# Attention and FFN in one kernel: score visits of three or four blocks, FFN tiles evicted once, and an order that keeps VectorE and GpSimd adds apart

## The chip, the core and the metric

The kernel runs on one core of a Trainium2 chip. TensorE (PE) multiplies matrices into PSUM, VectorE (DVE) and ScalarE (ACT) read PSUM and SBUF, GpSimd (POOL) reads SBUF, SyncE (SP) issues most DMAs. The metric is the device time of one launch in microseconds (us): the median of three runs.

## The reference

One layer, 2048 tokens of 640 values, no batch:

```python
xn = _layernorm(x, axis=-1)
return x + _A_ref(xn, A_wq, A_wk, A_wv, A_wo) + _B_ref(xn, B_w1, B_w2)
```

`_A_ref` is attention with 32 query heads of 20 values and one shared key and value head: `softmax(q k^T / sqrt(20)) v`, then `wo`. `_B_ref` is `silu(xn w1) w2` with 1728 hidden values.

## The kernel before, in words

**Tiling.** A score block is 128 keys by 512 queries of one head, transposed (keys on partitions). There are 4 chunks of 512 queries, 32 heads and 16 key tiles, so 2048 blocks. Four heads make a group, of 64 blocks; there are 32 groups. PSUM has eight banks of 512 fp32 columns. Two sets of three (banks 0 to 5) take score blocks in turn, bank 6 (`UBANK`) gathers the output of the group in work, bank 7 (`XBANK`) is the job bank: every other matmul tile of the loop goes through it, one at a time.

**A score visit** (`do_S`) multiplies three blocks side by side in row strips of PE (L823). ACT then exponentiates two of them in one instruction (L841), or all three. The third, where `want_dve` allows it, goes to DVE: a clamp from PSUM to 16-bit integers (L856, `p1`), whose bits read as bf16 approximate the exponential. Two more versions with an added constant refine it (`flush_z`): up to three clamped blocks make a set, the second version is made on POOL (L888), the first on DVE (L882) or POOL, by a comparison of their queues. So a DVE block costs three products with the values in place of one. A PV slot (`do_pv`, L762) multiplies one item for each of the four heads of the group, side by side in column strips of PE.

**Jobs** are the remaining matmul tiles: query tiles (`qd_job`, L977, emptied by DVE at L984), FFN first-layer tiles (`h_job`, L1013; ACT computes tanh of half the value at L1026, and DVE the product `(tanh + 1) * value` at L1031, both reading bank 7), FFN second layer and output projection (`out_job`, L1081 and L1086, emptied by DVE at L1098, L1104 or L1116). `fill_chunk` hands them out, with a first step each from `PACE` and `AHEAD`.

**Order.** The program is planned on the host. `Sched.run` simulates the five engines with fixed prices (`t_act`, `t_dve_ps` and others) and latencies, and writes down an order of instructions for each; the chip runs those lists, with semaphores for the data dependencies alone. On DVE, ACT and POOL the planner takes the ready instruction of the lowest `prio`. On PE, `step` chooses among a score visit (first, when its banks and operands are ready), a PV slot, a job matmul and a filling matmul of zeros; `PV_PRESS` and `PV_GO` say when PV comes first. A `lock`ed instruction of DVE isn't planned to start while a locked one of POOL runs, and the other way round; before, the DVE adds, normalisations and some of the start are locked, the POOL adds are not:

```python
        if op.lock:
            r = max(r, self.lock_end["pool" if op.eng == "dve" else "dve"])
```

**Start and end.** `prologue` loads x, computes the layer norm (statistics on DVE and ACT, norms on the engines of `NORM_ENG`), transposes it by DMA (tiles in `DT`, issued from SP) or on PE (`PRO`), and makes keys and values. After the last score block, leftover jobs and the last output projection remain.

Of the kernel before, what the change touches and what calls it, by code (L numbers as in the profile page):

```python
# [14 lines left out]
P = 128  # L15
# [32 lines left out]
ZB = 3  # L48
LATE_G = 0
AHEAD = 30  # L50
Q_FROM = 8
H0_STEP = 14
Y_SLOW = 0.1
# [4 lines left out]
ZWAIT = 6  # L58
SWITCH = 0.105
S_LEAD = 0.56  # L60
PV_PRESS = 8
DVE_TH = 3.4
U_PRIO = 1.1
X_PRIO = 0.8
PACE = (0.9, 0.9, 0.9, 0.9)
# [4 lines left out]
OVER = 0.1  # L70
PV_HOLD = 29
Q_EVERY = 2
DT_ISSUE = 1.28
UT_ISSUE = 1.05
DT = (4, 5, 6, 9, 10, 11, 12, 13, 14, 15)
NORM_P = 4.5
DVE_FROM = 8
NODB = 2
GB = 4 * KT
NB = NUNITS * KT  # L80
Y0_POOL = 1.0
Y0_COST = 1.45
YP_FIX = 0.14
YP_BLK = 0.47
PV_MIN = 4
PV_GO = 5
PRO = "v0 t7 t8 v1 k2 k3 k4 k5 v2 k6 k7 v3 q1 d0"
ACT_STATS = (4, 6, 9, 12, 14)
NW_ENG = ("dve", "dve", "dve")
NORM_ENG = ("pool", "pool", "pool", "pool", "act", "pool", "act", "act", "dve", "act", "act", "act")  # L90
# [256 lines left out]
def t_mm(n):  # L347
    return max(n, 64) / 2400.0 + 0.003
# [18 lines left out]
class Builder:  # L367
# [17 lines left out]
    def alloc(self):  # L385
# [21 lines left out]
        self.tb = sb([P, 2, QW], BF16)  # L407
        self.qo = sb([P, QW], BF16)
# [47 lines left out]
    def steps_init(self):  # L456
        self.NG = NUNITS // 4
        self.T = -(-NB // 3)
        self.s_next = 0
        self.misc = deque()  # L460
# [14 lines left out]
        self.cg = 0  # L475
        self.g_seen = [0] * self.NG
# [16 lines left out]
    def blocks(self, t):  # L493
        return [(b // GB, b % GB // 4, b % 4) for b in range(3 * t, min(3 * t + 3, NB))]

    def more(self):
        return (self.s_next < self.T or self.cg < self.NG or bool(self.misc) or bool(self.pro) or bool(self.urgent)
                or self.cur_job is not None)

    def bank_for_job(self, job=None):  # L500
# [8 lines left out]
        if self.s_next >= self.T:  # L509
            banks = [b for b in (7, 0, 1, 2, 3, 4, 5) if b not in self.heldb.values()]  # L510
# [31 lines left out]
    def s_reads(self, t, dv):  # L542
        k = []
        for g, kt, j in self.blocks(t):
            c, h = g // 8, 4 * (g % 8) + j
            k += [("kT1" if dv else "kT", kt // 2), ("kT", kt // 2), ("qb", c % 2, h)] + self.qkeys(c, h)
# [8 lines left out]
    def s_ready(self, t):  # L555
        r = self.reads_ready(self.s_reads(t, False))
# [4 lines left out]
        nh = len(self.blocks(t))  # L561
# [10 lines left out]
    def step(self, now):  # L572
        sc = self.sc
        t = self.s_next
        sr = INF
        if t < self.T:
            sr = self.s_ready(t)
            if sr <= now + 1e-9:
                self.do_S(t, now)
# [23 lines left out]
        if pv_n and (self.pe_mode == "PV" or press):  # L603
# [12 lines left out]
        if self.s_next >= self.T - LASTPV and (pv_n or self.s_next >= self.T and pv_some):  # L616
# [3 lines left out]
        if choice == "PV":  # L620
            d = 0.216 + self.switch("PV")
# [25 lines left out]
    def fill(self, now, until):  # L647
        if self.s_next >= self.T and self.cg >= self.NG:
# [936 lines left out]
```

## Time and profile before

| | before |
|---|---|
| time, median of three runs | 739.06 us (738.4 to 739.63) |
| profiled execution: time / span | 740.91 us / 738.9 us |
| busy of the span: PE, DVE, ACT, POOL | 709.2, 659.1, 695.0, 489.8 us |
| score exps (L841) | 683, 658.1 us |
| clamps (L856) | 653, 433.2 us |
| DVE adds (L882) / POOL adds (L888) | 150, 131.5 us / 292, 446.6 us |
| mean granted TensorE clock | 0.992 |

The span runs from the first to the last instruction of the core; the time holds the launch around it too. A group line gives the source line, engine, operation, what is written and read, the count, the busy time, the mean duration in ns, and the idle time of the engine just before with what ended it. Durations of neighbours on one engine overlap, so counts times means exceed what an engine needs. A wait line says who waited for whom, the total, the times, and the longest.

### The profile page before, as it was taken

The page shows a single profiled execution, that of the slowest core. Times are in us where ns is not written, and L with a number is a line of the kernel's source. Part 1 is how long each engine was busy: PE and PEld are TensorE (multiplying, and loading weights), DVE is VectorE, ACT ScalarE, POOL GpSimd, SP SyncE. Part 2 cuts the span into 40 slices and gives each one's busy share as a digit, 9 for nine tenths or more (in the row PEclk, how much of TensorE's full clock was granted, in tenths as well). Part 3 has the DMA queues.
Part 4 walks back from the last instruction along what each step waited for, and adds up shares of the span by engine and source line. Part 5 has one row for each costly group of instructions (what it writes and reads, how often), then busy time and mean ns, then how long its engine had stood idle before and what let it go on. Part 6 is the DMA issues. An engine that isn't in the chain of part 4 may idle for free.

```text
span 738.9 us, 17791 instructions
## 1 busy us (share of the span) xinstructions
PE 709.2 (96%) x6661; PEld 223.8 (30%) x6661; DVE 659.1 (89%) x1106; ACT 695.0 (94%) x775; POOL 489.8 (66%) x366
## 2 busy tenths in 40 slices
PE   9899999999999999999999999999999999999998
PEld 4422222233332322223333232222333223223334
DVE  6679989989998899999989899999998999999993
ACT  6979999999999999999999999999999999999990
POOL 3356766766777766767677676756775777566770
PEclk9979999999999999999999999999999999999999
DMA  9525310000010101000011011000001002000011
GB/s 283 113 84 154 110 15 19 12 16 16 9 45 9 43 25 34 20 19 8 8 11 43 8 59 37 16 16 16 8 2 43 10 8 62 27 8 1 9 37 36
DMA packets 52554, 27.69 MB, mean 37 GB/s; under 512 B 38422, under 2 KB 51830, under 8 KB 52470
## 3 DMA queue, kind: packets, MB, share of 16 engines
q1 hardware_dynamic: 51014, 26.35, 13.3%
q8 instruction: 54, 0.88, 0.5%
q10 hardware_dynamic: 1456, 0.22, 0.2%
q14 instruction: 30, 0.25, 0.1%
HBM read 11.44 MB, written 2.62 MB: 19 GB/s over the span
## 4 chain that ended last, share of the span: by engine, by line
PE 58%; DVE 19%; issue 11%; POOL 8%; ACT 3%; DMA 0%; POOLq 0%; DVEq 0%
PE psall L823 19%; PE psall L762 18%; DVE sbt L856 11%; PE psall L1081 9%; POOL sbt L888 8%; PE psall L1013 5%; DVE sbt L882 5%; PE psall L977 2%; PE psall L684 2%; PE psall L1086 1%; ACT sbt L841 1%; DVE sbt L1031 1%; ACT sbt L1362 1%; DVE sbt L931 1%; DVE sbt L1116 1%
## 5 line engine op out<-in xcount | busy, mean ns | idle before, releaser
L841 ACT ACTIVATE sbt<-psall 128x1024 bf16<-128x1024 f32 (+1 forms) x683 | 658.1, 1071 | 19.7 <-PE psall L823 16.3
L888 POOL TENSOR_TENSOR sbt<-sbt 128x768 int32<-128x768 int32 (+1 forms) x292 | 446.6, 1546 | 202.2 <-DVE sbt L856 158.6
L856 DVE TENSOR_SCALAR sbt<-psall 128x512 int16<-128x512 f32 x653 | 433.2, 682 | 49.0 <-PE psall L823 41.5
L823 PE MATMUL psall<-sbt 32*128 32x512 bf16 x2048 | 268.2, 386 | 15.9 <-DVE sbt L856 10.9
L762 PE MATMUL psall<-sbt 128*32 128x512 bf16 x3354 | 263.8, 386 | 4.6 <-DVE sbt L931 2.3
L823 PEld LDWEIGHTS psall<-sbt 32*128 32x128 bf16 x2048 | 68.2, 91 | 255.6 <-issue 98.0
L882 DVE TENSOR_SCALAR sbt<-sbt 128x1536 int16<-128x1536 int16 (+1 forms) x150 | 131.5, 876 | 2.7
L762 PEld LDWEIGHTS psall<-sbt 128*32 128x32 bf16 x3354 | 65.0, 94 | 119.4 <-issue 76.0
L1081 PE MATMUL psall<-sbt 128*128 128x320 bf16 x448 | 88.6, 303 | 0.0
L1013 PE MATMUL psall<-sbt 128*128 128x512 bf16 x260 | 79.2, 384 | 1.6 <-DVE sbt L1031 0.4
L1081 PEld LDWEIGHTS psall<-sbt 128*128 128x128 bf16 x448 | 34.3, 97 | 45.2 <-issue 33.1
L1031 DVE SCALAR_TENSOR_TENSOR sbt<-sbt,psall 128x512 bf16<-128x512 bf16 x54 | 36.6, 677 | 2.4 <-PE psall L823 1.1
L1026 ACT ACTIVATE sbt<-psall 128x512 bf16<-128x512 f32 x54 | 33.9, 628 | 0.2 <-DVE sbt L882 0.2
L977 PE MATMUL psall<-sbt 128*128 128x512 bf16 (+1 forms) x95 | 28.9, 385 | 0.6 <-DVE sbt L1031 0.6
L1086 PE MATMUL psall<-sbt 128*128 128x320 bf16 x144 | 29.1, 303 | 0.3 <-DVE sbt L1116 0.3
L920 POOL TENSOR_TENSOR sbt<-sbt 128x320 bf16<-128x320 bf16 x31 | 26.8, 865 | 3.8 <-DVE sbt L915 3.4
L1013 PEld LDWEIGHTS psall<-sbt 128*128 128x128 bf16 x260 | 17.1, 97 | 37.0 <-issue 22.2
L931 DVE CAST sbt<-psall 128x512 bf16<-128x512 f32 x32 | 21.8, 680 | 2.1 <-PE psall L762 2.1
L684 PE MATMUL psall<-sbt 128*128 128x512 bf16 (+2 forms) x76 | 20.3, 420 | 1.5 <-POOL sbt L1281 1.5
L1482 POOL TENSOR_SCALAR sbt<-sbt 128x256 bf16<-128x256 bf16 x8 | 4.1, 514 | 23.4 <-DVE sbt L1480 23.3
L1098 DVE SCALAR_TENSOR_TENSOR sbt<-psall,sbt 128x320 bf16<-128x320 f32 x28 | 13.5, 484 | 4.6 <-PE psall L1081 4.2
L1116 DVE SCALAR_TENSOR_TENSOR sbt<-psall,sbt 128x320 bf16<-128x320 f32 x28 | 13.2, 480 | 3.1 <-PE psall L1086 3.1
(81 smaller groups left out, 160.9 us busy)
## 6 DMA issues: line engine op xcount, KB each, us to landing
sbt<-in_A_x_dram SPq DMA_DIRECT2D x32, 160.0 KB, 3.4
out_dram<-sbt SPq DMA_DIRECT2D x15, 160.0 KB, 1.8
sbt<-in_B_w_dram SPq DMA_DIRECT2D x5, 432.0 KB, 6.3
sbt<-sbt SPq DMA_DIRECT2D x105, 20.0 KB
sbt<-in_B_w_dram SPq DMA_DIRECT2D x13, 160.0 KB, 3.0
sbt<-sbt SPq DMA_DIRECT2D x1, 1024.0 KB, 6.0
sbt<-sbt SPq DMA_TRANSPOSE x57, 2.4
sbt<-in_A_wo_dram SPq DMA_DIRECT2D x5, 160.0 KB, 2.7
```

The costliest lines, as they stand in the source:

```text
L684: return pe.matmul(self.bk(b, 0, n), self.zero[:, 0:P], self.zero[:, 0:n], start=True, stop=True)
L762: ins = pe.matmul(self.bk(UBANK, 0, QW, r, r + SLOT), self.v[:, it.w, it.kt, :], it.x(), start=f, stop=False, tile_position=(0, r), skip_g ...
L823: ins = pe.matmul(self.bk(par3 + i), self.kT[r:r + SLOT, kk, kt * P:(kt + 1) * P], self.qT[r:r + SLOT, g % 8, (g // 8) % 2, :], start=True ...
L841: return a.activation(self.E[:, b0 * QW:(b0 + na) * QW], self.ps[:, par3 * BANK:(par3 + na) * BANK], AF.Exp, scale=ACT_SCALE)
L856: return v.tensor_scalar(self.Z[:, zs, zp * QW:(zp + 1) * QW], self.bk(bb), 0.0, ZMAX, ALU.max, ALU.min)
L882: sc.new("dve", td, lambda v, k=k: v.tensor_scalar(self.Y[:, zs, k, 0:w], self.Z[:, zs, 0:w], float(PH[k + 1][0]), None, ALU.add), zk, yk, ...
L888: sc.new("pool", tp, lambda v, k=k, cb=cb: v.tensor_tensor(self.Y[:, zs, k, 0:w].bitcast(I32), self.Z[:, zs, 0:w].bitcast(I32), cb, ALU.ad ...
L977: return pe.matmul(self.bk(b, 0, QW, 0, rows), self.wq[:, k, lo:hi], self.xnT[:, k, c * QW:(c + 1) * QW], start=(k == 0), stop=(k == DC - 1))
L1013: return pe.matmul(self.bk(b), self.w1[:, k, fk * P:(fk + 1) * P], self.xnT[:, k, c * QW:(c + 1) * QW], start=(k == 0), stop=(k == DC - 1))
L1031: sc.new("dve", t_dve_ps(QW), lambda v: v.scalar_tensor_tensor(out=self.hT[0:rows, fk, :], in0=t, scalar=1.0, in1=src, op0=ALU.add, op1=AL ...
L1081: return pe.matmul(self.bk(b, 0, 320), self.hT[r0:r1, fk, i * P:(i + 1) * P], self.w2[r0:r1, fk, e0:e0 + 320], start=(m == 0), stop=(m == ...
L1086: return pe.matmul(self.bk(b, 0, 320), self.oT[:, k, i * P:(i + 1) * P], self.wo[:, k, e0:e0 + 320], start=(m == 0 and src != "ps"), stop= ...
```

## The change

A score visit takes a fourth block when the job bank is free, no job is open and at least one block of the four goes to DVE (`x_free`, `do_S`). `pick_dve` replaces `want_dve`: it may choose any of the visit's blocks, by how few blocks of that head DVE has taken (at most `TILE_CAP`), one in a visit of three and up to two in one of four, each below a bound on DVE's queue. In a visit of four, bank 7 holds a DVE block. The last two blocks of a group are no longer kept from DVE (`NODB` is 0).

An FFN tile is copied by DVE from bank 7 to a bf16 buffer `hb` in SBUF; tanh and the product read that buffer. POOL adds are locked as DVE adds are. A begun job goes on before PV (`JOB_BURST`). Sets are flushed after 3 visits in place of 6. In the start, the zero tile is set by DVE, tile 8 is transposed by DMA and tile 14 on PE, two norms leave ACT, and filling matmuls up to 5.6 us are priced at half speed. Prices, pacing and priorities of the planner are changed. What is left out below counts blocks (`bp`) and visits (`nv`) in place of steps.

```diff
@@ -47,47 +47,55 @@
-AHEAD = 30
-Q_FROM = 8
-H0_STEP = 14
-Y_SLOW = 0.1
+AHEAD = 31
+Q_FROM = 11
+H0_STEP = 18
+Y_SLOW = 0.085
-ZWAIT = 6
+ZWAIT = 3
-PV_PRESS = 8
+PV_PRESS = 2
-U_PRIO = 1.1
-X_PRIO = 0.8
-PACE = (0.9, 0.9, 0.9, 0.9)
+U_PRIO = 1.8856
+X_PRIO = 0.2256
+PACE = (0.85, 0.8, 0.75, 0.95)
-OVER = 0.1
-PV_HOLD = 29
-Q_EVERY = 2
+COLD = 5.6
+TILE_CAP = 10
+FOUR_FROM = 46
+JOB_BURST = 3
+TH_PRIO = 0.883
+DVE_TH2 = 0.562
+HP_PRIO = 5.8323
+FOUR_LAST = 4
+OVER = 0.0939
+PV_HOLD = 25
+Q_EVERY = 3
-DT = (4, 5, 6, 9, 10, 11, 12, 13, 14, 15)
-NORM_P = 4.5
-DVE_FROM = 8
-NODB = 2
+DT = (4, 5, 6, 8, 9, 10, 11, 12, 13, 15)
+NORM_P = 3.5
+DVE_FROM = 6
+NODB = 0
-Y0_POOL = 1.0
-Y0_COST = 1.45
-YP_FIX = 0.14
-YP_BLK = 0.47
+Y0_POOL = 1.1547
+Y0_COST = 1.5225
+YP_FIX = 0.185
+YP_BLK = 0.426
-PRO = "v0 t7 t8 v1 k2 k3 k4 k5 v2 k6 k7 v3 q1 d0"
+PRO = "v0 t7 k3 v1 k2 q1 k4 k5 v2 t14 k6 k7 v3 d0"
-NORM_ENG = ("pool", "pool", "pool", "pool", "act", "pool", "act", "act", "dve", "act", "act", "act")
+NORM_ENG = ("pool", "pool", "pool", "pool", "dve", "pool", "act", "act", "dve", "pool", "act", "act")
...
@@ -345,7 +353,7 @@
-    return max(n, 64) / 2400.0 + 0.003
+    return max(n, 64) / 2400.0 + (0.008 if n > 400 else 0.006 if n > 300 else 0.003)
...
         choice = None
-        if pv_n and (self.pe_mode == "PV" or press):
+        if JOB_BURST and job is not None and job.begun and not press:
+            choice = "M"
+        elif pv_n and (self.pe_mode == "PV" or press):
             choice = "PV"
...
-        if self.s_next >= self.T and self.cg >= self.NG:
+        if self.bp >= NB and self.cg >= self.NG:
-        room = min(until, now + 0.33) - now - self.switch(mode)
+        room = (min(until, now + (0.66 if now < COLD else 0.33)) - now - self.switch(mode)) / (2.0 if now < COLD else 1.0)
-        op = sc.new("pe", n / 2400.0 + self.switch(mode), fn, [("zero",)], [ukey] if ukey else [],
-                    name="fill", queue=False)
+        op = sc.new("pe", n / 2400.0 * (2.0 if now < COLD else 1.0) + self.switch(mode), fn, [("zero",)],
+                    [ukey] if ukey else [], name="fill", queue=False)
-        op.work = 0.216
+        op.work = 0.2215
...
@@ -792,46 +808,80 @@
         self.tq[g][tile].append(it)
         self.e_used += na
 
-    def want_dve(self, t):
-        g, kt, j = self.blocks(t)[-1]
-        if t < DVE_FROM or 4 * kt + j >= GB - NODB or t >= self.T - DVE_LAST:
-            return False
+    def pick_dve(self, bs, most):
+        t = self.s_next
+        if t < DVE_FROM or t >= self.T - DVE_LAST:
+            return []
         sc = self.sc
         back = sc.t["dve"] - sc.t["pe"]
         for op in sc.pend["dve"]:
             back += op.dur
         back += len(self.zblocks) * 0.6
-        return back < DVE_TH
-
-    def do_S(self, t, now):
+        got = []
+        cand = [x for x in bs if 4 * x[1] + x[2] < GB - NODB and self.nz[x[0]][x[2]] < TILE_CAP
+                and self.reads_ready([("kT1", x[1] // 2)]) <= sc.t["pe"] + 1e-9]
+        cand.sort(key=lambda x: (self.nz[x[0]][x[2]], -bs.index(x)))
+        for x, th in zip(cand, (DVE_TH, DVE_TH2)):
+            if back >= th or len(got) == most:
+                break
+            got.append(x)
+        return got
+
+    def x_free(self, now):
+        if self.cur_job is not None or not self.pv_started or self.pro_left:
+            return False
+        for d in self.sc.deps_of((), [("B", XBANK)]):
+            if d.avail is None or (d.avail if d.eng != "pe" else d.end) > now + 1e-9:
+                return False
+        return True
+
+    def do_S(self, now):
         sc = self.sc
-        bs = self.blocks(t)
-        nh = len(bs)
+        t = self.s_next
         self.started = True
         for c in range(QC):
             if c not in self.filled and t >= self.first_step[c] - AHEAD:
                 self.filled.add(c)
                 self.fill_chunk(c, t)
-        dv = self.want_dve(t)
-        par3 = 3 * (t % 2)
+        bs = self.blocks()
+        four = False
+        if len(bs) == 3 and t >= FOUR_FROM and t < self.T - FOUR_LAST and self.x_free(now):
+            b4 = self.blocks(4)
+            if len(b4) == 4 and self.reads_ready(self.s_reads(b4)) <= now + 1e-9:
+                dvs = self.pick_dve(b4, 2)
+                four = bool(dvs)
+        if four:
+            bs = b4
+        else:
+            dvs = self.pick_dve(bs, 1)
+        nh = len(bs)
+        par3 = 3 * (self.nv % 2)
+        acts = [x for x in bs if x not in dvs]
+        na = len(acts)
+        bank = {x: par3 + i for i, x in enumerate(acts)}
+        for x, bb in zip(dvs, (XBANK, par3 + na) if four else (par3 + na,)):
+            bank[x] = bb
 
         def fn(pe):
             ins = None
-            for i, (g, kt, j) in enumerate(bs):
+            for x in bs:
+                g, kt, j = x
                 r = j * SLOT
-                kk = 1 if (dv and i == nh - 1) else 0
-                ins = pe.matmul(self.bk(par3 + i), self.kT[r:r + SLOT, kk, kt * P:(kt + 1) * P],
+                kk = 1 if x in dvs else 0
+                ins = pe.matmul(self.bk(bank[x]), self.kT[r:r + SLOT, kk, kt * P:(kt + 1) * P],
                                 self.qT[r:r + SLOT, g % 8, (g // 8) % 2, :],
                                 start=True, stop=True, tile_position=(r, 0))
             return ins
-        op = sc.new("pe", 0.216 + self.switch("S"), fn, self.s_reads(t, dv), [("B", par3 + j) for j in range(nh)],
+        op = sc.new("pe", 0.216 + self.switch("S"), fn, self.s_reads(bs, dvs), [("B", bank[x]) for x in bs],
                     name=f"S{t}", queue=False)
         op.mm = nh
         op.work = 0.216
         self.pe_mode = "S"
-        self.s_next = t + 1
+        self.bp += nh
+        self.s_next = self.bp // 3 if self.bp < NB else self.T
+        v = self.nv
+        self.nv += 1
         sc.commit(op, now)
-        na = nh - 1 if dv else nh
         if self.blk_pos + na > NBLK:
             self.blk_pos = 0
         b0 = self.blk_pos
@@ -840,28 +890,31 @@
         def efn(a):
             return a.activation(self.E[:, b0 * QW:(b0 + na) * QW],
                                 self.ps[:, par3 * BANK:(par3 + na) * BANK], AF.Exp, scale=ACT_SCALE)
-        self.exp_op[t] = sc.new("act", t_act(na * QW), efn, [("B", par3 + j) for j in range(na)],
+        self.exp_op[v] = sc.new("act", t_act(na * QW), efn, [("B", par3 + j) for j in range(na)],
                                 [("E", b0 + j) for j in range(na)], prio=5.0, name=f"exp{t}")
-        for i in range(na):
-            g, kt, j = bs[i]
+        for i, (g, kt, j) in enumerate(acts):
             self.item(g, j, kt, 0, lambda b=b0 + i: self.E[:, b * QW:(b + 1) * QW], [("E", b0 + i)], 1)
             self.g_seen[g] += 1
-        if dv:
+        for x in dvs:
             self.dve_steps += 1
-            g, kt, j = bs[-1]
+            g, kt, j = x
+            self.nz[g][j] += 1
             zs, zp = self.zset, len(self.zblocks)
-            bb = par3 + nh - 1
-
-            def p1(v):
+
+            def p1(v, zs=zs, zp=zp, bb=bank[x]):
                 return v.tensor_scalar(self.Z[:, zs, zp * QW:(zp + 1) * QW], self.bk(bb), 0.0, ZMAX,
                                        ALU.max, ALU.min)
-            sc.new("dve", t_dve_ps(QW), p1, [("B", bb)], [("Z", zs, zp)], prio=1.0, name=f"p1_{t}")
-            self.item(g, j, kt, 0, lambda: self.Z[:, zs, zp * QW:(zp + 1) * QW].bitcast(BF16), [("Z", zs, zp)])
+            sc.new("dve", t_dve_ps(QW), p1, [("B", bank[x])], [("Z", zs, zp)], prio=0.9 if bank[x] == XBANK else 1.0,
+                   name=f"p1_{t}")
+            self.item(g, j, kt, 0, lambda zs=zs, zp=zp: self.Z[:, zs, zp * QW:(zp + 1) * QW].bitcast(BF16),
+                      [("Z", zs, zp)])
             self.g_seen[g] += 1
             self.g_late[g] += 1
-            self.zblocks.append((t, g, kt, j))
-        if self.zblocks and (len(self.zblocks) >= ZB or t - self.zblocks[0][0] >= ZWAIT or t == self.T - 1
-                             or 3 * (t + 1) >= GB * (self.zblocks[0][1] + 1)):
+            self.zblocks.append((v, g, kt, j))
+            if len(self.zblocks) >= ZB:
+                self.flush_z()
+        if self.zblocks and (v - self.zblocks[0][0] >= ZWAIT or self.bp >= NB
+                             or self.bp >= GB * (self.zblocks[0][1] + 1)):
             self.flush_z()
 
     def flush_z(self):
@@ -887,7 +940,7 @@
             cb = bass.AP(self.cy, c.offset, [list(c.ap[0]), [0, w // 2]])
             sc.new("pool", tp, lambda v, k=k, cb=cb: v.tensor_tensor(
                 self.Y[:, zs, k, 0:w].bitcast(I32), self.Z[:, zs, 0:w].bitcast(I32), cb, ALU.add), zk + [("cy",)], yk,
-                prio=4.0, name=f"yp{k}")
+                prio=4.0, name=f"yp{k}").lock = True
         for i, (t, g, kt, j) in enumerate(self.zblocks):
             for k in range(2):
                 self.item(g, j, kt, k + 1, lambda k=k, i=i: self.Y[:, zs, k, i * QW:(i + 1) * QW].bitcast(BF16),
@@ -1023,14 +1076,17 @@
             tp = fk % 2
             t = self.tb[0:rows, tp, :]
             src = self.bk(b, 0, QW, 0, rows)
-            sc.new("act", t_act(QW), lambda a: a.activation(t, src, AF.Tanh, scale=0.5), [("B", b)], [("tb", tp)],
-                   prio=X_PRIO, name=f"th{c}_{fk}")
+            hb = self.hb[0:rows, tp, :]
+            sc.new("dve", t_dve_ps(QW), lambda v: v.tensor_copy(hb, src), [("B", b)], [("hb", tp)], prio=X_PRIO,
+                   name=f"hc{c}_{fk}")
+            sc.new("act", t_act(QW), lambda a: a.activation(t, hb, AF.Tanh, scale=0.5), [("hb", tp)], [("tb", tp)],
+                   prio=TH_PRIO, name=f"th{c}_{fk}")
             ks = [("hT", fk)]
             if c == 0:
                 ks += [("hT_x", i) for i in range(fk * QW // D, min(self.XS - 1, (fk * QW + QW - 1) // D) + 1)]
-            sc.new("dve", t_dve_ps(QW), lambda v: v.scalar_tensor_tensor(
-                out=self.hT[0:rows, fk, :], in0=t, scalar=1.0, in1=src, op0=ALU.add, op1=ALU.mult),
-                [("B", b), ("tb", tp)], ks, prio=X_PRIO, name=f"hp{c}_{fk}")
+            sc.new("dve", t_dve_1x(QW), lambda v: v.scalar_tensor_tensor(
+                out=self.hT[0:rows, fk, :], in0=t, scalar=1.0, in1=hb, op0=ALU.add, op1=ALU.mult),
+                [("hb", tp), ("tb", tp)], ks, prio=HP_PRIO, name=f"hp{c}_{fk}")
...
-        pool(0.3, lambda g: g.memset(self.zero[:, :], 0.0), [], [("zero",)])
+        np_("dve", 0.3, lambda v: v.memset(self.zero[:, :], 0.0), [], [("zero",)], prio=-1.0, name="zero")
```

## The prediction

> **What bounds the kernel now.** I read the page's busy shares first, then its chain and groups by shape, then the waits, then stretches of the timeline.
>
> ```profile
> PE 709.2 (96%) x6661; PEld 223.8 (30%) x6661; DVE 659.1 (89%) x1106; ACT 695.0 (94%) x775; POOL 489.8 (66%) x366
> ...
> PE 58%; DVE 19%; issue 11%; POOL 8%; ACT 3%; DMA 0%; POOLq 0%; DVEq 0%
> ```
>
> Three engines are nearly full and the chain runs through all of them, so a change must relieve PE, ACT and DVE together. The groups by shape give the prices:
>
> ```profile
> L841 ACT ACTIVATE sbt<-psall 128x1024 bf16<-128x1024 f32 x654 | 620.9, 1053 | 19.0 <-PE psall L823 15.9 <-ACT sbt L841 0.4
> L856 DVE TENSOR_SCALAR sbt<-psall 128x512 int16<-128x512 f32 x653 | 433.2, 682 | 49.0 <-PE psall L823 41.5 <-POOL sbt L888 0.9
> L888 POOL TENSOR_TENSOR sbt<-sbt 128x768 int32<-128x768 int32 x280 | 432.9, 1563 | 198.9 <-DVE sbt L856 155.3 <-PE psall L823 26.4 <-issue 4.1
> ...
> L882 DVE TENSOR_SCALAR sbt<-sbt 128x1536 int16<-128x1536 int16 x142 | 123.8, 872 | 2.5
> ...
> L841 ACT ACTIVATE sbt<-psall 128x1536 bf16<-128x1536 f32 x29 | 42.0, 1466 | 0.6 <-PE psall L823 0.5
> L1031 DVE SCALAR_TENSOR_TENSOR sbt<-sbt,psall 128x512 bf16<-128x512 bf16 x54 | 36.6, 677 | 2.4 <-PE psall L823 1.1 <-ACT sbt L1026 1.0
> L1026 ACT ACTIVATE sbt<-psall 128x512 bf16<-128x512 f32 x54 | 33.9, 628 | 0.2 <-DVE sbt L882 0.2
> ```
>
> Durations overlap their neighbours, so I price by median start-to-start times of back-to-back instructions, taken from the trace: exp of two blocks 0.904 us, of three 1.330; clamp (L856) 0.601; eviction of 512 columns (L931) 0.598; tanh 0.477; silu product (L1031) 0.595. From the exps, a block costs ACT 0.426 and a visit 0.052 more. So the number of visits hardly matters to ACT; the number of blocks that DVE takes does.
>
> From the first exp (17.8 us after the first instruction) to the last (720.5), ACT needs 654x0.904 + 29x1.330 + 54x0.477 + some 8 of prologue work = 664 of 702 us; 38 are lost to waits. PE, counted as columns/2400 plus the 0.105 us that the trace shows at each change between scores, PV and other matmuls, has in its usual 50 us about 36 of work, 11 of changes and 3 of idle time. DVE from 60 to 720: 535 us of demand at these prices, plus about 51 because its adds (L882) take 0.82 start to start where they could take 0.47: 587 of 660.
>
> The waits name the couplings: score visits wait for the clamp that frees their bank, the exps for the score visits.
>
> ```profile
> PEld psall L823 <- DVE sbt L856: 71.2, 162, 1.2
> PEld psall L823 <- ACT sbt L841: 52.3, 132, 1.3
> ...
> ACT sbt L841 <- PE psall L823: 16.3, 35, 1.5
> ...
> PEld psall L762 <- POOL sbt L888: 13.3, 43, 0.8
> ```
>
> Two stretches of the timeline show what the change touches.
>
> ```profile
> 227.66 0.82 PE L1013 MATMUL psall<-sbt 128*128 128x512 bf16 x3
> ...
> 228.84 0.62 ACT L1026 ACTIVATE sbt<-psall 128x512 bf16<-128x512 f32 x1
> ...
> 230.06 0.68 DVE L1031 SCALAR_TENSOR_TENSOR sbt<-sbt,psall 128x512 bf16<-128x512 bf16 x1
> ```
>
> ```profile
> 254.94 2.89 POOL L888 TENSOR_TENSOR sbt<-sbt 128x768 int32<-128x768 int32 x2
> ...
> 256.49 1.76 DVE L882 TENSOR_SCALAR sbt<-sbt 128x1536 int16<-128x1536 int16 x1
> ```
>
> First: an FFN tile's last matmul is followed by tanh and product, and bank 7 is free at 230.74 only. Second: a DVE add that begins inside a GpSimd add ends 0.42 after that one.
>
> **The change, part by part.**
>
> *Job bank and four-block visits.* Between 60 and 718 us, from a job's first matmul to the end of the instruction that empties it, bank 7 is held for 592 us. An FFN tile holds it 2.60 us after its last matmul, a query tile, with one eviction, 1.49. The copy brings the first to the second: 52x1.1 = 57 us. Jobs of 14 matmuls (29 of them) hold it 6.7 us while filling; with a begun job kept before PV, a visit cadence of 1.03 us leaves some 0.6 us in each for 0.136 us matmuls, so 3.3 us: 98 more. Free time becomes 66 + 57 + 98 = 221 us. A fourth block holds the bank about 1.25 us: at most 170 four-block visits, at least a handful, if the next job always begins first. I take 100, as a visit and a job compete for each free moment. Then 33 visits fall away, on PE 33x(0.216 + 2x0.105) = 14 us, on ACT 33x0.052 = 1.7.
>
> *Bursts.* The trace has 123 changes between PV and job matmuls; I take 80 away, 8 us of PE. Single-tile PV slots (34, 0.22 each) may fall with the cap of 10 blocks per tile: 4 more. PE in all: -26, and +2 for the PV of 17 more DVE blocks.
>
> *Who takes the blocks.* 21 of the 29 three-block exps lie at the end of a group, which the exclusion of its last two blocks explains; it goes: +20 blocks on DVE. Fewer visits: -33. A second block per visit needs a DVE backlog under 0.562 us, seldom there: +30. Net +17 (from -20 to +60). ACT: -17x0.426 = -7.2; DVE: +17x0.6 = +10 and +3 for adds.
>
> *The copy.* DVE: 54x0.598 = +32.3. Tanh now reads SBUF: a 640-column pass from SBUF takes 0.626 to 0.642 start to start (L1327, L1330), from PSUM 0.592 (L1461), so about +0.04x54 = +2.2 of ACT; ends 0 and +11.8 (L1362's 0.811, whose scale and bias are per row). The product now has both inputs in SBUF. No row shows that at this size. Below: L1367's 640 columns in 0.354 would save 17 us. Above: if it stalls like a DVE add inside a GpSimd one (91 of 142 began so, 1.049 us against 0.556) it costs 0.49 x 54 = +26. The present product lasts 677 ns inside GpSimd work and 678 outside, but one input is PSUM; I take half the upper end, +13. It now comes after the adds; only the FFN's second half reads it, many us later, though two buffers of the copy mean that the tile after next waits for it.
>
> The Trainium skill's page "SBUF — State Buffer" (section "SBUF: two separate sides") speaks against this step: a DVE instruction with two SBUF inputs takes the port pair that GpSimd uses, and whichever starts first blocks the other entirely. By that rule the product costs the whole +26, and with a third of the extra 13 on the path the sum below would be 4 us longer; the L882 lines show the blocking for a one-input add, none here for two inputs.
>
> *Adds apart.* 91x0.49 = 45 us of DVE stalls. The lock exists in the planner only; at run time nothing enforces it, and orders drift. I take -30 (ends 0 and -45). With DVE's queue longer, its rule sends more first adds to GpSimd: 29 of 150, -16 of DVE, +42 of GpSimd, whose idle time is 200. GpSimd adds wait up to 0.56 for DVE's: PV waits of 13.3 us could double; I take +3. The flush after 3 visits makes more two-block sets, whose GpSimd add costs 1.17 against two thirds of 1.46: 0.2 each, hidden in the same idle time. DVE in all: 10 + 3 + 32 + 13 - 30 - 16 = +12, 599 of then 640 us: 94% where it was 89%.
>
> *Start and end.* Two norms leave ACT (one to DVE, one to GpSimd): -1.6 where ACT works back to back. Transposes by DMA stay ten, tile 8's in place of 14's on SP's queue; keys of tile 8 may come later (ends 0 and +2, taken 0, as waits for DMA there are 0.4 us). The zero memset moves to DVE, idle to 3.14 us; fills start sooner, before data arrive: nothing, and were DVE busy there, its 0.53 us. Query and FFN pacing (AHEAD, PACE, H0_STEP, Q_FROM, Q_EVERY) changes where jobs stand, not how many; the new prices of matmuls and adds, and the priorities, change the planner's picture alone and are taken at nothing beyond the counts above, with either sign possible within the range. At the end, jobs left over run from 722.6 to 728.7 alone on PE, 6.1 us; relief on PE lets some finish earlier: -3 (0 to -6).
>
> *Sum*, against the profiled execution's 740.91 (span 738.9 and 2.0 around it): ACT work -7.2 - 1.7 + 2.2 - 1.6 = -8.3. Its 38 us of waits: PE loses 24 us of 676, which would end most waits for scores, but DVE's room shrinks; -11, and +3 for late adds: -8. End -3. Together 721.6; the median of the three runs is 1.85 below the profiled one: 720 (719.8).
>
> **Rivals.**
> - *DVE becomes the bound (slower).* If copies (32), stalled products (26) and 10 for clamps come and the adds don't come apart, 68 of the 73 idle us are gone. A third on the path, 23, plus late adds 3 against ACT's -8.3 and PE waits unchanged: 740.9 + 18 - 1.9 = 757; with half of the 45 us of separation, 7 less: 750. It decides once DVE's demand grows by about 40 us, which takes it to 95% of its 660, where ACT stands now (664 of 702). For it: no wait enforces the order. Against: GpSimd has room for first adds.
> - *The fourth block seldom finds the bank.* For: 592 of 658 us held, and gaps between jobs of 0.43 us median. With 20 such visits only separation, norms, bursts and some waits remain: 740.9 - 6 - 1.9 = 733.
> - *DVE has more room than I give it.* Separation in full and products without stalls leave 28 us for 35 more blocks: 15 of ACT, so 705. For it: GpSimd's 200 idle us.
>
> **How the numbers follow.** Forecast 0.50 (own range 710 to 729), more room 0.18, seldom free 0.11, bound by DVE 0.16, nothing measurable 0.05. The range 702 to 744 leaves out the low end of the second (0.06) and most of the slower case (0.12). About 0.2% is what a measurement here can tell. Faster 0.79, same 0.05, slower 0.16.
>
> **What the profile after would show.** Right: some 650 exps, some 670 clamps, DVE adds near 0.6 us, 54 new evictions in 0.68, ACT idle in the loop below 30 us. Wrong: products of 1 us or more, more score waits on DVE, fewer than 650 clamps, or over 670 exps. I'd be wrong most easily on how long DVE can run at 94% without holding up the score visits.

## The result and the profile after

The changed kernel takes 732.97 us (median of four runs, 732.01 to 733.77) where the kernel before takes 739.06: a ratio of 0.9917, 95% interval 0.9900 to 0.9935. I forecast 720. The sign was right and the size was not: 6 us came where 19 were forecast, and the time lies inside the range only through its upper part.

The page after, busy shares and chain:

```profile
PE 693.6 (95%) x6623; PEld 221.4 (30%) x6623; DVE 665.3 (91%) x1126; ACT 693.8 (95%) x741; POOL 526.9 (72%) x394
...
PE 57%; DVE 21%; issue 10%; ACT 8%; POOL 4%; DMA 0%; DVEq 0%; POOLq 0%; ACTq 0%
```

PE is busy 16 us less, ACT only 1, DVE 6 more. Groups by shape (busy us, mean ns, idle time before):

```profile
L891 ACT ACTIVATE sbt<-psall 128x1024 bf16<-128x1024 f32 x550 | 529.1, 1071 | 15.6 <-PE psall L871 12.4 <-PE psall L778 2.2
L941 POOL TENSOR_TENSOR sbt<-sbt 128x768 int32<-128x768 int32 x299 | 459.7, 1555 | 160.9 <-DVE sbt L905 131.6 <-PE psall L871 15.2 <-PE psall L778 6.8
L905 DVE TENSOR_SCALAR sbt<-psall 128x512 int16<-128x512 f32 x645 | 430.0, 683 | 48.0 <-PE psall L871 39.8 <-POOL sbt L941 1.2
...
L891 ACT ACTIVATE sbt<-psall 128x1536 bf16<-128x1536 f32 x101 | 149.5, 1485 | 3.5 <-PE psall L871 3.2
...
L935 DVE TENSOR_SCALAR sbt<-sbt 128x1536 int16<-128x1536 int16 x109 | 76.4, 703 | 0.8
...
L1087 DVE SCALAR_TENSOR_TENSOR sbt<-sbt 128x512 bf16<-128x512 bf16 x54 | 64.5, 1197 | 1.2 <-ACT sbt L1082 1.0
L1080 DVE CAST sbt<-psall 128x512 bf16<-128x512 f32 x54 | 36.6, 679 | 0.1
L1082 ACT ACTIVATE sbt<-sbt 128x512 bf16<-128x512 bf16 x54 | 36.2, 670 | 2.7 <-DVE sbt L1080 2.6
```

There are 651 score visits, 96 of them of four blocks, much as forecast. DVE's adds came apart in part (872 to 703 ns; 45 of 109 still begin inside a GpSimd instruction, 91 of 142 before). But the product of the FFN tile (L1087), 677 ns before, takes 1197; and 101 exps have three blocks where 29 had.

The start, the loop (first exp to last exp) and the end, in us from the first instruction, which stands at 0.24 us in the timelines below:

| | before | after |
|---|---|---|
| first exp begins | 17.8 | 15.5 |
| loop | 702.7 | 703.7 |
| last exp to last instruction | 15.7 | 9.9 |
| last instruction ends | 736.2 | 729.1 |

The whole gain lies in the start and the end; the loop, which the change rewrites, is not shorter. For the end, PE's longest stretches of job matmuls behind the last score block, before (L1081, the FFN's second layer) and after (L1142, the output projection):

```profile
724.30 2.17 PE L1081 MATMUL psall<-sbt 128*128 128x320 bf16 x14
...
726.63 2.17 PE L1081 MATMUL psall<-sbt 128*128 128x320 bf16 x14
```

```profile
721.53 1.40 PE L1142 MATMUL psall<-sbt 128*128 128x320 bf16 x9
```

Before, tiles of 14 matmuls still run alone on PE after the last score block; after, only the output projection does. For the start, PE's queue up to the transposes, before (windows of 0 to 7.5 and 8 to 14 us) and after (0 to 18 us):

```profile
1.46 6.21 PE L684 MATMUL psall<-sbt 128*128 128x512 bf16 x15 [1.46 <-POOL sbt L1281]
...
7.73 5.13 PE L684 MATMUL psall<-sbt 128*128 128x512 bf16 x23
12.69 1.28 PE L1453 MATMUL psall<-sbt 128*128 128x128 bf16 x20
```

```profile
1.19 9.36 PE L700 MATMUL psall<-sbt 128*128 128x512 bf16 x30 [1.19 <-DVE sbt L1337]
10.39 1.28 PE L1509 MATMUL psall<-sbt 128*128 128x128 bf16 x20
```

Before, the transposes (L1453) stood in PE's queue behind 39 filling matmuls (L684). The planner had priced each at 0.213 us; the first 15 took 0.41 us each, those from 7.73 us on 0.22. Now 30 stand there (L700).

Within the loop, PE needs 7 us less for score slots, 4 for PV and 4 for changes between kinds of matmul (37 fewer of 0.105 us), and 6 more for the tiles that no longer wait for the end. By this count, an estimate with some matmul records missing, its idle time grew by some 10 us.

### The profile page after: what moved, and what is told of

The parts are those of the page before. It is cut to its first block, busy times and chain, and to the rows that moved or that the text cites. A ratio compares the mean times of both kernels' runs of the same rounds, so it can differ in the third digit from the quotient of the medians.

```text
span 731.9 us, 17627 instructions
## 1 busy us (share of the span) xinstructions
PE 693.6 (95%) x6623; PEld 221.4 (30%) x6623; DVE 665.3 (91%) x1126; ACT 693.8 (95%) x741; POOL 526.9 (72%) x394
## 4 chain that ended last, share of the span: by engine, by line
PE 57%; DVE 21%; issue 10%; ACT 8%; POOL 4%; DMA 0%; DVEq 0%; POOLq 0%; ACTq 0%
PE psall L778 19%; PE psall L871 18%; DVE sbt L905 10%; PE psall L1137 9%; ACT sbt L891 7%; POOL sbt L941 4%; DVE sbt L1087 4%; PE psall L1066 4%; PE psall L1142 2%; DVE sbt L935 2%; PE psall L1030 2%; DVE sbt L1080 2%; PE psall L700 1%; ACT sbt L1082 1%; DVE sbt L984 1%
## 5 line engine op out<-in xcount | busy, mean ns | idle before, releaser
L891 ACT ACTIVATE sbt<-psall 128x1024 bf16<-128x1024 f32 (+1 forms) x651 | 655.9, 1135 | 19.1 <-PE psall L871 15.7
L941 POOL TENSOR_TENSOR sbt<-sbt 128x768 int32<-128x768 int32 (+1 forms) x320 | 482.9, 1527 | 163.9 <-DVE sbt L905 134.2
L871 PE MATMUL psall<-sbt 32*128 32x512 bf16 x2048 | 255.3, 385 | 21.9 <-DVE sbt L905 10.8
L935 DVE TENSOR_SCALAR sbt<-sbt 128x1536 int16<-128x1536 int16 (+1 forms) x122 | 83.1, 683 | 0.9
L1066 PE MATMUL psall<-sbt 128*128 128x512 bf16 x260 | 75.7, 384 | 3.6 <-DVE sbt L1080 1.4
L1087 DVE SCALAR_TENSOR_TENSOR sbt<-sbt 128x512 bf16<-128x512 bf16 x54 | 64.5, 1197 | 1.2 <-ACT sbt L1082 1.0
L1137 PEld LDWEIGHTS psall<-sbt 128*128 128x128 bf16 x448 | 33.9, 97 | 46.6 <-issue 35.1
L1082 ACT ACTIVATE sbt<-sbt 128x512 bf16<-128x512 bf16 x54 | 36.2, 670 | 2.7 <-DVE sbt L1080 2.6
L1080 DVE CAST sbt<-psall 128x512 bf16<-128x512 f32 x54 | 36.6, 679 | 0.1
L1142 PE MATMUL psall<-sbt 128*128 128x320 bf16 x144 | 28.8, 303 | 2.3 <-DVE sbt L1172 1.8
L1066 PEld LDWEIGHTS psall<-sbt 128*128 128x128 bf16 x260 | 17.8, 97 | 37.7 <-issue 19.2
L984 DVE CAST sbt<-psall 128x512 bf16<-128x512 f32 x32 | 21.8, 680 | 0.4 <-PE psall L778 0.4
L700 PE MATMUL psall<-sbt 128*128 128x512 bf16 (+3 forms) x57 | 15.9, 435 | 1.2 <-DVE sbt L1337 1.2
L1142 PEld LDWEIGHTS psall<-sbt 128*128 128x128 bf16 x144 | 11.2, 97 | 18.3 <-issue 8.3
```

The lines of the kernel that those rows point to most:

```text
L871: ins = pe.matmul(self.bk(bank[x]), self.kT[r:r + SLOT, kk, kt * P:(kt + 1) * P], self.qT[r:r + SLOT, g % 8, (g // 8) % 2, :], start=True, ...
L891: return a.activation(self.E[:, b0 * QW:(b0 + na) * QW], self.ps[:, par3 * BANK:(par3 + na) * BANK], AF.Exp, scale=ACT_SCALE)
L935: sc.new("dve", td, lambda v, k=k: v.tensor_scalar(self.Y[:, zs, k, 0:w], self.Z[:, zs, 0:w], float(PH[k + 1][0]), None, ALU.add), zk, yk, ...
L941: sc.new("pool", tp, lambda v, k=k, cb=cb: v.tensor_tensor(self.Y[:, zs, k, 0:w].bitcast(I32), self.Z[:, zs, 0:w].bitcast(I32), cb, ALU.ad ...
L1066: return pe.matmul(self.bk(b), self.w1[:, k, fk * P:(fk + 1) * P], self.xnT[:, k, c * QW:(c + 1) * QW], start=(k == 0), stop=(k == DC - 1))
L1080: sc.new("dve", t_dve_ps(QW), lambda v: v.tensor_copy(hb, src), [("B", b)], [("hb", tp)], prio=X_PRIO, name=f"hc{c}_{fk}")
```

## The experiments

Ratios are to the kernel before, timed beside each run on the same chip (medians 740.3 to 740.7); the changed kernel's is 0.9917. All but two of these are planned anew, so the whole order shifts; one control gives one case of what that alone does.

**Undo one part each.**

Without the copy:

```diff
-            sc.new("dve", t_dve_ps(QW), lambda v: v.tensor_copy(hb, src), [("B", b)], [("hb", tp)], prio=X_PRIO, ...)
-            sc.new("act", t_act(QW), lambda a: a.activation(t, hb, AF.Tanh, scale=0.5), [("hb", tp)], [("tb", tp)], ...)
+            sc.new("act", t_act(QW), lambda a: a.activation(t, src, AF.Tanh, scale=0.5), [("B", b)], [("tb", tp)], ...)
...
-                out=self.hT[0:rows, fk, :], in0=t, scalar=1.0, in1=hb, op0=ALU.add, op1=ALU.mult),
+                out=self.hT[0:rows, fk, :], in0=t, scalar=1.0, in1=src, op0=ALU.add, op1=ALU.mult),
```

> The changed kernel with FFN tiles as before: tanh and product read the job bank, no copy. It is planned anew and has 92 visits of four and 653 clamps (the changed kernel has 96 and 645). Theory 1, the port theory: the gain in the loop was lost on VectorE, to 54 copies of 0.6 us and to products of 1.16 us start to start in place of 0.6, 62 us together. Then this is faster than the changed kernel (732.97): 724 to 729. Rival, the bank theory: the copy is what lets jobs and fourth blocks through bank 7, so without it jobs come late and the end grows again: 736 to 741.

Measured 731.17, ratio 0.9869 (0.9850 to 0.9888). Neither theory: the loop is 16 us shorter (687.3) and the end 14 longer (23.7). The end of its timeline:

```profile
710.80 8.50 PE L1134 MATMUL psall<-sbt 128*128 128x320 bf16 x56
719.23 2.35 PE L1139 MATMUL psall<-sbt 128*128 128x320 bf16 x16
```

Four tiles' worth of second-layer matmuls run alone after the last score block. So the copy does what it is for, letting jobs through bank 7, and its price in the loop is about what it saves at the end. Whether the shorter loop is more than deferred work is asked further down.

Product locked in the planner:

```diff
-                [("hb", tp), ("tb", tp)], ks, prio=HP_PRIO, name=f"hp{c}_{fk}")
+                [("hb", tp), ("tb", tp)], ks, prio=HP_PRIO, name=f"hp{c}_{fk}").lock = True
```

> The changed kernel with the product locked in the planner against GpSimd's adds, as VectorE's adds are. 634 clamps in place of 645, so 4.7 us more for ScalarE. Theory 1: products fall from a mean of 1.2 us to below 0.8, VectorE gets some 25 us back, half of it is given to ScalarE's extra blocks: 729 to 733. Rival: order alone can't hold two engines apart at run time, products stay above 1.1 us and the time rises to 735 to 739.

Measured 746.83, ratio 1.0094 (1.0074 to 1.0114). Its products:

```profile
L1087 DVE SCALAR_TENSOR_TENSOR sbt<-sbt 128x512 bf16<-128x512 bf16 x54 | 59.3, 1112 | 0.0
```

Still 1112 ns. The planned order did not keep the product out of GpSimd's instructions: 34 of the 54 begin inside one. The time lies above both of my ranges. Why this plan costs so much is not shown; its granted clock is lower too, 0.984 to 0.989 in its runs against 0.994 to 0.998 in the changed kernel's.

Visits of three only:

```diff
-FOUR_FROM = 46
+FOUR_FROM = 10000
```

> The changed kernel with visits of three only: 683 visits, 662 clamps, 20 exps of three blocks (651, 645 and 101 in the changed one). If PE sets the loop's pace, 32 more visits cost 14 us of PE and the time is 738 to 745. Rival, ScalarE sets it: its exps need 626 us against 632, and the time is 727 to 732.

Measured 753.47, ratio 1.0170 (1.0150 to 1.0189). With the copies in, the fourth block is worth some 19 us, more than PE's 14: ScalarE's demand is lower (626 us) and yet the loop takes 722.5, with 45 us of idle time on ACT where the changed kernel has 22. The ScalarE theory falls. How much of the loss comes from pacing that was set for visits of four is not shown.

GpSimd adds not locked:

```diff
-                prio=4.0, name=f"yp{k}").lock = True
+                prio=4.0, name=f"yp{k}")
```

> The changed kernel without the lock on GpSimd's adds: 656 clamps, 114 VectorE adds and 330 GpSimd adds (645, 122, 320 in the changed one). Theory 1: VectorE's adds go back from 0.68 to some 0.87 us and products stay long, 20 us and more of VectorE, and the time is 736 to 742. Rival: the adds' order matters little, since the product's stall is the larger; the 11 more clamps take 4.7 us from ScalarE and the time is 729 to 733.

Measured 755.26, ratio 1.0196 (1.0180 to 1.0213). The adds:

```profile
L935 DVE TENSOR_SCALAR sbt<-sbt 128x1536 int16<-128x1536 int16 x107 | 94.8, 886 | 1.8
```

886 ns in place of 703 (69 of 107 begin inside a GpSimd instruction), 20 us of DVE, and a loss beyond the range that I gave it.

**A control.**

```diff
-DVE_TH = 3.4
+DVE_TH = 3.3
```

> A control: the changed kernel with the bound on VectorE's queue (DVE_TH) at 3.3 in place of 3.4. Nearly the same plan: 651 visits, 97 of four, 642 clamps, 119 VectorE adds (651, 96, 645, 122). If differences between plans mean what I take them to mean, the time stays within 3 us of 732.97: 730 to 736. Rival, the sensitivity theory: each plan anew lands anywhere within some 15 us, since the constants were fitted to one plan, and the large losses of the runs without the fourth block, without the lock and with the locked product are mostly this: then 738 to 755 here too.

Measured 729.93, ratio 0.9860 (0.9841 to 0.9878), better than the changed kernel by 0.6%. A new plan can move the time by at least so much, and differences of that size between planned kernels say nothing of an edit. The losses of 2.5% without the fourth block and 2.8% without the lock stand out against it, the 1.8% of the locked product less so. Part of what such a plan shifts can be seen in its adds and products, which are held up less (703 and 1197 ns in the changed kernel); its loop is 5.4 us shorter.

```profile
L935 DVE TENSOR_SCALAR sbt<-sbt 128x1536 int16<-128x1536 int16 x107 | 66.7, 625 | 0.7
...
L1087 DVE SCALAR_TENSOR_TENSOR sbt<-sbt 128x512 bf16<-128x512 bf16 x54 | 59.4, 1101 | 1.6 <-ACT sbt L1082 1.2
```

**Does the copy's price in the loop go away with a job-first rule?** Without copies (first), and with copies in the last two chunks (second):

```diff
         if self.cur_job is not None or not self.pv_started or self.pro_left:
             return False
+        if self.s_next >= 341 and self.misc and self.job_ready(self.misc[0]) < INF:
+            return False
```

> No copy of FFN tiles, and from visit 341 on no fourth block while the next job could start: 668 visits, 45 of four, 663 clamps; in the plan 18 second-layer and output matmuls of this form stand behind the last score block, where the kernel without copies had 118 and the changed one has 24. Bank theory: without copies the loop runs as there (687 us from first to last exp, some 5 more for 16 more visits on PE) and the end is as short as in the changed kernel (10 us): 717 to 724. Rival: the loop of the kernel without copies was short only because it left its jobs to the end, so with the jobs in it the loop is as long as in the changed kernel: 731 to 738.

> Copies for the FFN tiles of the last two query chunks only, and from visit 600 on no fourth block while a job could start: 656 visits, 82 of four, 653 clamps, 64 second-layer matmuls behind the last score block. Port theory: half the copies and stalled products, 31 us of VectorE less than in the changed kernel, loop about 695; the end 5 us longer: 727 to 732. Rival as above: 733 to 740.

```diff
+            cp = c >= 2
+            if cp:
                 hb = self.hb[0:rows, tp, :]
...
+        if self.s_next >= 600 and self.misc and self.job_ready(self.misc[0]) < INF:
```

Measured 731.58, 0.9873 (0.9856 to 0.9890); and 732.18, 0.9888 (0.9871 to 0.9904). The rival holds for the first: the end is short (9.2 us) and the loop is back at 700.1. The short loop without copies was mostly deferred work. The second lies between its two ranges, with a loop of 695.7 and an end of 16.3, and decides nothing. Taken further, with hardly a fourth block:

```diff
+        if self.misc and self.job_ready(self.misc[0]) < INF:
+            return False
```

> No copies, and a fourth block only when no job could start, which leaves 5 of them: 681 visits, 674 clamps, 18 matmuls of the second layer and output behind the last score block. It differs from the kernel before by the lock, the start, the choice of blocks and the constants. PE theory: 13 more visits than the run with 45 fourth blocks (731.6), 6 us of PE: 735 to 740. ScalarE theory: exps need 621 us in place of 625: 726 to 730.

Measured 730.76, 0.9863 (0.9845 to 0.9882), between my two ranges. With 92, 45 and 5 visits of four, kernels without copies take 731.2, 731.6 and 730.8: there the fourth block brings nothing that can be told from the control's 0.6%.

**One part alone.** The price of filling matmuls in the kernel before:

```diff
-        room = min(until, now + 0.33) - now - self.switch(mode)
+        room = (min(until, now + (0.66 if now < COLD else 0.33)) - now - self.switch(mode)) / (2.0 if now < COLD else 1.0)
...
```

> The kernel before with one edit, the price of filling matmuls in the first 5.6 us at half speed, so fewer of them. Start theory: the transposes on PE begin 2 us sooner, the first exp at about 15.6 us in place of 17.8, and the time falls by 2 to 3: 737 to 738.5 where the kernel before takes 740.3. Rival: the plan behind it differs, and the loop swallows or multiplies it: 740 or more, or 734 or less.

Measured 740.49, 1.0004 (0.9992 to 1.0015). The first exp begins at 15.3, as the start theory has it, so this edit makes the earlier start; but the loop behind it is 3.8 us longer, within what a new plan does.

The lock in the kernel before:

```diff
-                prio=4.0, name=f"yp{k}")
+                prio=4.0, name=f"yp{k}").lock = True
```

> The kernel before with the lock on GpSimd's adds alone: 652 clamps, 147 VectorE adds, 295 GpSimd adds, visits of three. Separation theory: the mean of VectorE's adds falls from 0.87 us to 0.70 or less, 25 us of VectorE, and the time falls to 730 to 737 (740.5 for the kernel before). Rival: the lock makes adds late as often as it saves a stall: 739 to 746.

Measured 733.85, 0.9912 (0.9896 to 0.9929).

```profile
L882 DVE TENSOR_SCALAR sbt<-sbt 128x1536 int16<-128x1536 int16 x141 | 104.0, 742 | 0.7
```

One word in one line gives what the whole change gives. The adds fall from 872 to 742 ns and the loop from 702.7 to 695.2. Both together:

> The kernel before with two edits, the lock on GpSimd's adds and the price of the first filling matmuls: 652 clamps, 143 VectorE adds, 72 matmuls behind the last score block. If the start's 2.4 us and the lock's 6.7 are separate gains: 730 to 732.5 (733.9 with the lock alone). Rival: as with the price alone, the loop behind it takes it back or overdoes it: 734 or more, or 728 or less.

Measured 732.57, 0.9898 (0.9879 to 0.9917), just above the first range and 1.3 us below the lock alone. The intervals of the two runs overlap, so a separate gain of the start in the whole time is not shown.

**The same order, the product's wait taken away.** These two runs keep every engine's order; 52 of the 54 products are another instruction, statistics of 512 values of the tanh tile in the first and of 64 (`t[:, 0:64]`) in the second. The kernels leave out those products, so their result is not the layer's.

```diff
-                out=self.hT[0:rows, fk, :], in0=t, scalar=1.0, in1=hb, op0=ALU.add, op1=ALU.mult),
+                out=self.hT[0:rows, fk, :], in0=t, scalar=1.0, in1=hb, op0=ALU.add, op1=ALU.mult) if pair else v.bn_stats(
+                self.scr[:, tp, :], t[:, 0:512]),
...
```

> The changed kernel with every instruction of every engine in the same order, but 52 of the 54 FFN products are replaced by statistics of 512 values of the tanh tile (one SBUF input, six results), so the FFN is not computed. Such an instruction takes 0.473 us for 320 values in the start of both traces, so some 0.65 us here, where the product takes 1.2. Port theory: the wait of a two-input product for GpSimd is gone, 28 us of VectorE with the plan untouched, and a third to two thirds of that lies on the path: 714 to 724. Rival: VectorE has 56 idle us in the loop anyway, the loop is set by PE and by the plan, and the time stays at 730 to 734.

> As the run with 512 values, but the statistics are of 64 values, some 0.2 us: another 24 us of VectorE taken from the same plan. If VectorE's lateness is what holds the loop, another 8 to 14 us: 704 to 714. If the first step took all that lies on the path: within 3 us of it. Rival: 730 to 734.

Measured 717.58, 0.9687 (0.9670 to 0.9705), and 715.87, 0.9662 (0.9644 to 0.9681).

```profile
L1089 DVE BATCH_NORM_STATS2 sbt<-sbt 128x6 f32<-128x512 bf16 x52 | 35.5, 685 | 2.9 <-ACT sbt L1083 2.8
```

The replacement takes 685 ns, about as long as the product before the change (677). With 52 x 0.51 = 27 us less on DVE in an unchanged plan, the time falls by 2.3% of 740, 17 us. Of the 52 statistics 43 begin inside a GpSimd instruction and still take 686 ns. That they also write less does not explain it: of the clamps, which write 512 values from one input in PSUM, 476 of 645 begin inside a GpSimd instruction and take 684 ns there, 682 elsewhere. Statistics of 64 values, 24 us of DVE less again (218 ns each), bring 0.25% more, and the intervals of the ratios overlap. So it is the product's wait that cost the loop its gain; its work, shortened once the wait is gone, gives next to nothing. Shortening the work with the wait in place was not tried. Kernels without copies stood at 0.986 to 0.987, this plan with the copies and without the wait at 0.969: across plans, and so as an estimate, the copy pays and the wait takes it back.

The timeline shows the wait, here a GpSimd add and a product of the changed kernel:

```profile
72.78 1.46 POOL L941 TENSOR_TENSOR sbt<-sbt 128x768 int32<-128x768 int32 x1 [2.00 <-DVE sbt L905]
73.26 1.53 DVE L1087 SCALAR_TENSOR_TENSOR sbt<-sbt 128x512 bf16<-128x512 bf16 x1
```

The add ends at 74.24, the product 0.55 later. Of the 54 products 46 begin inside a GpSimd instruction, and their ends lie 0.55 us behind its end in nearly every case (5th to 95th percentile 0.548 to 0.553); the other 8 take 0.67 us. GpSimd is held up too: 27 of its adds of three blocks begin inside a product, and they end 1.32 us after the product's end (1.316 to 1.326) and take 1.89 us on the mean. Before, 17 began inside a product with one input in PSUM and took 1.46. With the statistics, GpSimd is busy for 15 us less (511.9 us), so the 17 us above hold that side of the wait as well.

**More blocks for VectorE, and shorter GpSimd instructions.**

```diff
-DVE_TH2 = 0.562
+DVE_TH2 = 2.0
```

> The changed kernel with the queue bound for a visit's second VectorE block (DVE_TH2) at 2.0 us in place of 0.562: 72 visits of four with two VectorE blocks in place of 7, 691 clamps in place of 645, and 94 second-layer and output matmuls behind the last score block in place of 24. It asks whether my count of VectorE blocks (17 more than before, where there were 8 fewer) was what the forecast failed on. ScalarE theory: exps need 611 us in place of 632, the loop falls by up to 20, the end grows by 9: 718 to 726. VectorE theory: 46 more clamps and 12 more adds are 34 us for an engine that is already late, the loop doesn't fall, and with the end it is 738 to 755.

Measured 763.04, 1.0306 (1.0280 to 1.0332). Score visits wait for clamps more (64.5 us in the changed kernel), and ACT for score visits:

```profile
PEld psall L871 <- DVE sbt L905: 96.4, 235, 1.8
...
ACT sbt L891 <- PE psall L871: 43.6, 55, 2.8
```

ACT has 20 us less to do and idles 32 us longer in the loop (54 against 22). With copies and waiting products in the kernel, more blocks for DVE, 46 here where my count had 25 more than came, do not give the time.

```diff
-            sc.new("pool", tp, lambda v, k=k, cb=cb: v.tensor_tensor(
...
+            for b0, b1 in ((0, 2), (2, 3)) if n == 3 else ((0, n),):
+                sc.new("pool", YP_FIX + YP_BLK * (b1 - b0), lambda v, k=k, cb=cb, b0=b0, b1=b1: v.tensor_tensor(
...
+                    ALU.add), zk[b0:b1] + [("cy",)], yk[b0:b1], prio=4.0, name=f"yp{k}").lock = True
```

> The changed kernel with each GpSimd add of three blocks made in two instructions, of two blocks and of one, about 1.00 and 0.60 us in place of 1.42. 650 clamps, 97 visits of four, 37 matmuls behind the last score block (24 before this edit). Port theory: a product or a VectorE add waits for the rest of one GpSimd instruction, so the mean product falls from 1.20 to 1.0 us or less, and the time falls to 724 to 730 (733 for the changed kernel). Rival: GpSimd, with some 50 us more to do, is late with its versions, and the time is 734 to 745.

Measured 724.71, 0.9786 (0.9766 to 0.9806): 1.3% better than the changed kernel and the best of the runs that compute everything. It is 0.7% better than the control, hardly more than a new plan can do, so the size of this gain is not settled.

```profile
L943 POOL TENSOR_TENSOR sbt<-sbt 128x512 int32<-128x512 int32 x336 | 365.3, 1091 | 79.4 <-DVE sbt L905 58.1 <-PE psall L871 9.8 <-issue 4.3
L943 POOL TENSOR_TENSOR sbt<-sbt 128x256 int32<-128x256 int32 x311 | 209.5, 675 | 3.8 <-DVE sbt L905 1.9 <-PE psall L871 0.9 <-PE psall L778 0.3
...
L1089 DVE SCALAR_TENSOR_TENSOR sbt<-sbt 128x512 bf16<-128x512 bf16 x54 | 53.6, 993 | 2.6 <-ACT sbt L1084 1.9 <-DVE sbt L905 0.2
```

More products begin inside a GpSimd instruction (51), but its rest is 0.46 us long on the mean and not 0.74; the product falls to 993 ns. DVE's own adds gain nothing (771 ns where they took 703). GpSimd is busy for 75 us more (601.5 against 526.9), out of idle time. The loop is 692.2.

## Why the prediction was right or wrong

- **Visits of four and PE's relief: right in count.** 100 forecast, 96 there; 651 exps where I had 650; PE's score slots 7 us less, PV 4. The bursts were wrong: I took 80 changes between PV and jobs away, and the trace has 163 where it had 123.
- **Who takes the blocks: wrong.** +17 blocks on DVE forecast, -8 came. I expected 30 visits with a second DVE block; 7 of the 96 have one, so 89 visits of four leave three blocks to ACT. ScalarE's exps need 631.5 us and not 621 (629.8 before). But the pricing behind the step was wrong too: in the run with 46 more blocks on DVE, none of ACT's 0.426 us a block came back in the time.
- **The copy: the wait was mis-sized.** The step "the product now has both inputs in SBUF" took half of its upper end, 13 us of DVE; it is 30 (54 x (1.160 - 0.597), start to start), beyond that end. I weighed the present product's 677 against 678 ns as evidence, and it has one input in PSUM. The rule of the Trainium skill that I named there (page "SBUF — State Buffer", section "SBUF: two separate sides") is what the 46 products show, to 0.55 us behind the end of GpSimd's instruction, and the 27 GpSimd adds show it the other way round. Tanh from SBUF: 0.523 us against 0.477, +2.5 where I had +2.2.
- **Adds apart: right.** DVE's adds shed 48 us of busy time (131.5 to 83.1) where I had 46 of separation and moved adds, and the lock alone is worth the whole change.
- **DVE in all: right by luck.** +12 forecast; clamps -5, copies +32, products +30, adds -48 give +9. What failed is the next step, that this leaves ACT's 38 us of waits 8 shorter: in the loop they are 37 (703.7 less 631.5 of exps, 28 of tanh and 6.5 of the start's work). A third of added DVE time on the path was too little for a product that stands still: 17 us of time for 27 of DVE, with 15 of GpSimd, in the run with the order kept.
- **The sum.** ScalarE's work in the loop grew by some 3 us where I had 8.3 less, which is 11 of the 13 us between 720 and 733. Its waits fell by 1 or 2 where I had 8, which is some 6 more. Start and end gave 5 more than I had. So two terms failed: the blocks that DVE was to take, and the waits that were to shrink while DVE had room. The runs show what stood behind the second, a product held up in 46 of 54 cases; that its wait is worth 17 us, more than the whole miss, is shown for the changed kernel's order alone.
- **Start: wrong.** The new price of the filling matmuls, and so fewer of them, was in the sum at nothing, among prices that "change the planner's picture alone". The first norms were done by 11 us and the transposes stood behind the fills until 12.69: 2.3 us, in the lines of the timeline before.
- **End: right in kind,** 5.8 us where I had 3.
- **Rivals.** DVE as the bound was half right: its stalled products came in full, its separation came too, and the two met near zero. That the bank is seldom free gave 733, the measured time, for another reason: the bank was free, for 96 visits. That the time equals this rival's is luck.
- **Signs.** Of those that the prediction named for being wrong, products above 1 us and fewer than 650 clamps (645) came; more score waits on DVE (64.5 us where there were 71.2) and over 670 exps did not.

## What to carry to other kernels

Before an operand moves to SBUF, look whether the instruction then has two inputs there and what GpSimd does meanwhile; a copy that frees a bank can hand its cost to the instruction behind it. Undo the parts of a change one by one and beside a control that only shakes the plan: here the lock alone gave as much as the whole change, and the rest came out even in sum. An experiment that keeps the order and swaps one instruction tells far more than one that plans anew.

## What the runs showed of the hardware

- A two-input product from SBUF (128x512, bf16) that begins inside a GpSimd instruction ends 0.55 us after that one's end, in nearly all of 46 cases of the changed kernel; outside it takes 0.67. One-input statistics over the same tile take 0.69 in the same places, and the product with one input in PSUM 0.68.
- It goes the other way too: a GpSimd add (128x768, int32) that begins inside such a product ends 1.32 us after it, in all of 27 cases, and takes 1.89 us where it took 1.46 inside a product with one input in PSUM.
- Shorter GpSimd instructions shorten the other engine's wait: with adds of 1.56 us split into 1.09 and 0.68, the product's mean falls from 1.20 to 0.99 us. GpSimd is busy for 75 us more, and the kernel is 1.3% faster than the changed one, 0.7% faster than the control.
